# Scales from sums of squares by a product with ones, and half of w_in's sums split in place

## The chip, the cores and the metric

The kernel runs on one core of a Trainium2 chip. The metric is the device time of one execution in microseconds. A core has five engines with a queue of instructions each, which run in order: PE (TensorE, matrix products, with PEld for its weight loads), DVE (VectorE), ACT (ScalarE), POOL (GpSimd) and SP (SyncE, which here only issues DMAs). They wait for one another through semaphores. PSUM holds the results of products, SBUF the operands.

## The reference, cut to what matters

```python
scores = scale * (q @ k.T)                       # 4 batches, 8 heads, 576 rows, 64 wide
scores = where(scores >= max(scores) - tau, scores, -1e9)
x = softmax(scores) @ v                          # 2304 tokens, 512 wide
x = ((x @ w1) * (x @ w2)) @ w3 @ w_out           # moe, 1024 wide inside
h = x @ w_in                                     # moe2, 2048 wide inside
out = where(h > 0, h, exp(min(h, 0)) - 1) @ w_out2
```

## The kernel before

The kernel has five stages, one after the other, with overlap at their ends: attention, with the two products a and b of the first MoE and g = a·b (to 468 us); M = w3·w_out of the first MoE as one matrix (to 513); **the x2 stage**, x2 = g·M (to 630); and **MoE2** (to 1022).

The weights come in as 64-bit numbers. A chunk of 128 x 1024 is converted in four operations, which `conv_ops` gives: `top` on ACT, `rest` and `sign` (bit operations) and `join` on DVE. A product in full precision is three products of halves: a tile is split into a high half, a rounded copy, and a low half, the difference. For 16-bit halves the tile is first scaled by a power of two, which depends on its largest element. The scales are numbers that all 128 partitions need, while a maximum over a row gives one number for each partition.

Before the change a maximum over partitions is made by `everywhere` (L984): SP stores the column to DRAM (`mx_dr`, L988), loads it back as a row into every partition (`mxb`, L991), and DVE reduces it (L994). `power` (L978) makes a power of two of it.

The x2 stage runs over NB = 6 blocks of 384 tokens (the order is `JS`) and NK = 4 parts of 128 columns: 24 units with 24 products each (L1321), with x2 in PSUM (`x2`, four buffers). After the fourth unit of a block the g of the next block is split, in eight parts on ACT (`sl`, L325) and eight on DVE (L326), and the g of the block after that is loaded by SP (`th` from `g_dr`, L1128). ACT copies each x2 unit, the first eight into `bq` (L1361), the others into one of two buffers `x2s` (L1364), which SP stores (L1365). `x_size` (L1200) takes the maximum of a unit on DVE. `sums`, `high_b` and `low_b` make the sums of x2 quarters that MoE2's scheme needs and split them (`tq`, `so`).

Beside this, `win_jobs` converts w_in in eight chunks, in four pairs q. Each pair gives seven matrices (four of them sums, `s1` to `s4`, made on GpSimd in `both`), and SP stores all seven to DRAM (`wi_dr`, L1241). `size` takes the chunk's maximum on DVE (L1265). A list of jobs is worked off, one or two after each unit. At the stage's end the scale of all of w_in is made, again by `everywhere`.

MoE2 multiplies 2 x 2 blocks by seven products where eight would be needed. It runs in 24 steps s = (p, f): p is one of three thirds of the tokens, f one of eight parts of w_in. A step has seven products h (L1482), each of six matmuls; ACT takes the first from PSUM (`m1`, L1523), DVE adds up the others (`sum_of`, L1508), elu is made from the sums on ACT and DVE (L1409 to L1420), and the results are kept for the output products o (L1433), which fill in five at a time behind each product of the next step. In the first eight steps the parts of w_in come from DRAM: SP loads `wr`, GpSimd scales it (L1304), ACT makes the high half (L1307), GpSimd the low one (L1310), two at a time from `after`. In steps 0 to 3 four chunks of the last w_out are converted as well (`wo_steps`, with the maximum at L1021, the scaled copy at L1031 and its halves at L1032 and L1033). At step 4 their largest maximum is read (`seen`), and `h_scale` sets the scales of all three thirds.

The order on each engine is that of the program; nothing reorders it behind.

## Time and profile before

| | |
|---|---|
| median of three runs | 1027.48 us (1025.41 to 1027.63) |
| profiled execution | 1027.93 us, span 1026.1 us |
| PE busy | 948.0 us, 92% |
| PEld busy | 693.3 us, 68% |
| DVE busy | 778.3 us, 76% |
| ACT busy | 549.3 us, 54% |
| POOL busy | 444.2 us, 43% |
| mean granted clock of TensorE | 0.982 |

The span runs from the first instruction to the last; the execution's own time is 1.8 us more. A share of busy time is a mean over stages which have different limits. So the rows below are read by stage: how long a stage took, how long each engine was busy in it, and, on the engine that was idle, what ended its wait. In the chain that ended last each step is followed back to what released it. [...]

### The profile page before, as it was taken

Reading aid. Unit: us, or ns where it says so; the run is one execution under the profiler, and the core shown is the slowest. Engines: PE = TensorE matmul, PEld = TensorE weight load, DVE = VectorE, ACT = ScalarE, POOL = GpSimd, SP = SyncE. Lnnn points to the kernel's source line nnn. Section 1 sums busy time; section 2 is a strip of 40 time slices with the busy share of each in tenths; the row PEclk is TensorE's granted clock in tenths of the full one; section 3 lists DMA queues with packets and bytes.
Section 4 is the critical chain, followed back from the end, with each engine's and each line's share of the span. In section 5 each row is a group of like instructions: output and inputs, shape, how many; then the busy total and the mean of one; then the engine's idle time right before and its main releaser. Section 6 shows DMA issues by size and latency. Waiting matters only on the chain. (4 is left out here: it accounts for less than half of the span.)

```text
span 1026.1 us, 17137 instructions
## 1 busy us (share of the span) xinstructions
PE 948.0 (92%) x6074; PEld 693.3 (68%) x6074; DVE 778.3 (76%) x1448; ACT 549.3 (54%) x945; POOL 444.2 (43%) x608
## 2 busy tenths in 40 slices
PE   7889999989899999999999687687799999999998
PEld 4456788868799998997799686343355555555554
DVE  6889876888678785788968574888788677776664
ACT  5877776877666674454544233455455333443333
...
GB/s 261 148 129 168 153 156 141 169 169 176 179 203 185 202 135 160 280 214 263 206 180 268 158 198 226 154 124 36 60 31 1 124 2 1 1 63 1 1 1 62
DMA packets 167282, 138.18 MB, mean 135 GB/s; under 512 B 118332, under 2 KB 153884, under 8 KB 162588
## 3 DMA queue, kind: packets, MB, share of 16 engines
...
## 5 line engine op out<-in xcount | busy, mean ns | idle before, releaser
L681 PE MATMUL ab<-x,W 128*128 128x256 f32 (+1 forms) x1536 | 223.8, 298 | 6.3 <-DVE g L696 5.2
L1482 PE MATMUL h<-so,WI 128*128 128x384 f16 x1008 | 196.6, 333 | 32.1 <-DVE th L1508 18.6
L681 PEld LDWEIGHTS ab<-x,W 128*128 128x128 f32 x1536 | 207.6, 188 | 15.5 <-DVE g L696 6.2
L1433 PE MATMUL o<-WO,gg 128*128 128x512 f16 x864 | 214.3, 381 | 0.0
L1482 PEld LDWEIGHTS <-WI 128*128 128x128 f16 x1008 | 100.0, 99 | 121.3 <-issue 39.6
L1508 DVE SCALAR_TENSOR_TENSOR th<-h,back,th 128x384 f32<-128x384 f32 x168 | 100.8, 613 | 72.6 <-PE h L1482 72.0
L1433 PEld LDWEIGHTS <-gg 128*128 128x128 f16 x864 | 84.9, 98 | 86.0 <-issue 2.1
L526 DVE SCALAR_TENSOR_TENSOR e<-s,st,e 128x576 f32<-128x576 f32 x144 | 115.2, 808 | 24.1 <-ACT e L520 22.4
L537 POOL TENSOR_TENSOR hl<-e,hl 128x512 f16<-128x512 f32 x94 | 110.8, 1179 | 24.9 <-ACT hl L533 18.4
L502 DVE TENSOR_REDUCE st<-s 128x1 f32<-128x576 f32 x144 | 106.0, 750 | 17.5 <-PE s L492 10.1
L1321 PE MATMUL x<-sl,M 128*128 128x384 f32 x576 | 105.7, 346 | 11.1 <-ACT sl L325 4.4
L1410 ACT ACTIVATE et<-et 128x384 f32<-128x384 f32 x96 | 49.1, 511 | 120.7 <-DVE et L1409 120.7
L1321 PEld LDWEIGHTS x<-sl,M 128*128 128x128 f32 x576 | 103.7, 195 | 13.0 <-ACT sl L325 4.7
L1415 ACT ACTIVATE gg<-th,c_by 128x384 f16<-128x384 f32 x96 | 58.9, 613 | 74.0 <-DVE th L1413 73.8
L520 ACT ACTIVATE e<-s,st 128x576 f32<-128x576 f32 x108 | 78.4, 737 | 25.5 <-POOL st L510 16.6
L492 PE MATMUL s<-qk 128*128 128x288 f32 x480 | 83.1, 306 | 5.3 <-DVE e L526 4.4
L492 PEld LDWEIGHTS s<-qk 128*128 128x128 f32 x480 | 67.9, 189 | 14.0 <-issue 7.7
L533 ACT ACTIVATE hl<-e 128x576 f16<-128x576 f32 x94 | 63.1, 681 | 23.6 <-DMA pt<-hl 10.9
L1413 DVE SCALAR_TENSOR_TENSOR th<-et,th 128x384 f32<-128x384 f32 x96 | 59.4, 618 | 14.8 <-ACT et L1410 14.2
L1420 DVE SCALAR_TENSOR_TENSOR gg<-th,c_by,gg 128x384 f16<-128x384 f32 x96 | 62.9, 655 | 0.2 <-ACT gg L1415 0.2
L1310 POOL TENSOR_TENSOR WI<-wr,WI 128x256 f16<-128x256 f32 x56 | 41.9, 748 | 22.7 <-ACT WI L1307 22.7
L480 PE MATMUL s<-qkp 128*64 128x288 f32 x288 | 42.2, 427 | 7.1 <-ACT pt L578 3.7
...
## 6 DMA issues: line engine op xcount, KB each, us to landing
...
```

What stands on the lines that cost most here:

```text
L492: T.matmul(s[:, n, :HS], q, k[:, c:c + HS], start=(x == 0), stop=(x == len(ops) - 1))
L502: V.tensor_reduce(st[i][:, 0:1], sc[i][:, :, :HS], axis=AX.XY, op=ALU.max if plain else ALU.min, negate=plain)
L520: A.activation(et[i], sc[i][:, :, :HS], AF.Exp, bias=st[i][:, k:k + 1], scale=esc if plain else -1.0)
L526: V.scalar_tensor_tensor(et[i], sc[i][:, :, :HS], st[i][:, 1:2], et[i], op0=ALU.is_ge if p < NPL else ALU.is_le, op1=ALU.mult, accum_out=s ...
L533: A.activation(hl[i][:, :S], et[i].rearrange("p a b -> p (a b)"), AF.Copy)
L537: G.tensor_tensor(t[:, S + 64:], e[:, :512], t[:, :512], op=ALU.subtract)
L681: T.matmul(o[:, :w], wf[:, m, wx, kt, :], x[:, xx, :], start=(kt == 0 and k == 0), stop=(kt == NK - 1 and k == 2),)
L1321: T.matmul(o[:, :TB], M[:, f, mx, e * P:(e + 1) * P], gh[j, f][:, gx, :], start=(k == 0), stop=(k == 23),)
L1420: V.scalar_tensor_tensor(h[:, 1, :], x, c["by"], h[:, 0, :], op0=ALU.mult, op1=ALU.subtract)
L1433: T.matmul(po[j, t], dst["h"][:, gx, t * P:(t + 1) * P], WO[f // 2 % 4][:, f // 8, f % 2, wx, :], start=(first and k == 0), stop=(stop and ...
L1482: T.matmul(o[:, :TB], w[:, wx, kt, :], bs[k][:, kt, xx, :], start=(i == 0), stop=(i == 5),)
L1508: V.scalar_tensor_tensor(x, a, back[:, p:p + 1], b, op0=ALU.mult, op1=ALU.add)
```

## The change

- A scale is no longer made of a maximum, but of the root of a sum of squares: `root` halves the exponent of the sum. `square` makes a chunk's sum, on ACT for the first chunk of a pair of w_in and for w_out, on DVE for the second of a pair. `x_size` is a square on ACT, in place in PSUM, with a sum.
- The sum over partitions is a product with a matrix of ones (`total`), which lands in unused columns of a PSUM tile that is in use; DVE reads it after the next unit or product. `everywhere` stays for the maximum of w_out's scales, twice, with its load apart from its store.
- Each pair q of w_in has a scale of its own. For q = 0 and 1 (f = 0 to 3) `direct` splits the seven matrices where they stand, in the x2 stage: ACT copies with scale into the high half, DVE makes the low half one unit behind. They are no longer stored to and loaded from DRAM, nor scaled on GpSimd. For q = 2 and 3 the way is the old one, with five splits a step.
- The jobs of the x2 stage have fixed units (`slot`). One more chunk of w_out is converted there; three are left for steps 0 to 3. GpSimd's low half of a w_out chunk comes later (`behind`).
- The last maximum of w_out is read after the second product of step 4 and not ahead of its first sum; the scales of the second and third third of the tokens are made in step 5.

The diff, cut to its core:

```diff
+        def square(o, eng):
+            x, u = c["w"].bitcast(F32), c["u"]
+            if eng is A:
+                A.activation(u, x, AF.Square, accum_out=o)
+            else:
+                V.scalar_tensor_tensor(u, x, 1.0, x, op0=ALU.mult, op1=ALU.mult, accum_out=o)
+
+        return [top, rest, sign, join, high, low, lambda: c["w"].bitcast(F32), square]
...
-    def power(o, x, floor, by):
-
-        V.tensor_scalar(o.bitcast(I32), x.bitcast(I32), 0x7F800000, None, op0=ALU.bitwise_and)
-        V.tensor_scalar(o, o, floor, by, op0=ALU.max, op1=ALU.mult)
+    def root(o, x, floor, by):
+
+        V.tensor_scalar(
+            o.bitcast(I32), x.bitcast(I32), 1, 0x7F800000, op0=ALU.logical_shift_right, op1=ALU.bitwise_and
+        )
+        V.tensor_scalar(o, o, by * 2.0 ** 64, by * floor, op0=ALU.mult, op1=ALU.max)
 
     def everywhere(x):
 
@@ -986,14 +1004,15 @@
         nr[0] += 1
         d = drp.tile([P, k], F32, name=f"mx_dr{n}")
         SP.dma_start(d, x)
-        t = rawp[0].tile([P, 2 * P], F32, tag="mxb", name=f"mxb{n}", bufs=1)
-        flat = d.rearrange("(o p) k -> o (p k)", o=1)
-        SP.dma_start(t[:, :P * k], flat.to_broadcast([P, P * k]))
+        t = rawp[0].tile([P, P], F32, tag="mxb", name=f"mxb{n}", bufs=1)
+
+        def load():
+            SP.dma_start(t[:, :P * k], d.rearrange("(o p) k -> o (p k)", o=1).to_broadcast([P, P * k]))
 
         def read(o):
             V.tensor_reduce(o, t[:, :P * k].rearrange("p (a k) -> p k a", k=k), axis=AX.X, op=ALU.max)
 
-        return read
+        return load, read
...
-            V.tensor_reduce(raw_[:, c], ops[6](), axis=AX.X, op=ALU.max, apply_absolute_value=True)
-            power(two[:, c], raw_[:, c], LEAST, 2.0 ** -13)
+            root(two[:, c], raw_[:, c], LEAST, 2.0 ** -13)
             V.reciprocal(to[:, c], two[:, c])
...
-            G.tensor_tensor(t[:, :, 1, :], x2, t[:, :, 0, :], op=ALU.subtract)
-
-        return [[ops[0], ops[1]], [ops[2]], [ops[3], size], [halves]]
+            behind.append(lambda: G.tensor_tensor(t[:, :, 1, :], x2, t[:, :, 0, :], op=ALU.subtract))
+            if q % 4 < 2:
+                lows()
+
+        def lows():
+            while behind:
+                behind.pop(0)()
+
+        return [
+            [ops[0], ops[1], lows], [ops[2]], [ops[3], lambda: ops[7](raw_[:, c], A)], [size, halves]
+        ]
...
     def x_size(x, e, o):
-        V.tensor_reduce(xm[:, 4 * x + e:4 * x + e + 1], o, axis=AX.X, op=ALU.max, apply_absolute_value=True)
-
-    def x_sizes(p, o):
-        V.tensor_reduce(o, xm[:, 8 * p:8 * p + 8], axis=AX.X, op=ALU.max)
+        A.activation(o, o, AF.Square, scale=ROOM, accum_out=xm[:, 4 * x + e:4 * x + e + 1])
+
+    def total(o, x):
+
+        T.matmul(o[:, TB:TB + x.shape[1]], ones, x, start=True, stop=True)
+
+        def read(t, n):
+            V.tensor_reduce(
+                t, o[:, TB:TB + x.shape[1]].rearrange("p (n k) -> p n k", n=n), axis=AX.X, op=ALU.add
+            )
+
+        return read
...
+    def w_scale(q):
+        t = slice(q, q + 1)
+        root(w_two[:, t], wg[:, t], LEAST, 1.0)
+        V.tensor_scalar(w_to[:, t], w_two[:, t], 2.0 ** -11, None, op0=ALU.mult)
+        V.reciprocal(w_to[:, t], w_to[:, t])
...
+        def direct(k):
+            if q not in WIP:
+                WIP[q] = wp.tile([P, 2, NC, 2, 256], F16, tag=f"W{4 + 2 * q}", name=f"WI{q}")
+                for s_ in range(2):
+                    WI[2 * q + s_] = WIP[q][:, s_].rearrange("p k x (t c) -> p k x t c", t=2)
+            t, x, by = WIP[q][:, :, k], c[names[k]], w_to[:, q:q + 1]
+            A.activation(t[:, :, 0, :], x, AF.Copy, scale=by)
+            while behind:
+                behind.pop(0)()
+            behind.append(lambda: V.scalar_tensor_tensor(
+                t[:, :, 1, :], x, by, t[:, :, 0, :], op0=ALU.mult, op1=ALU.subtract
+            ))
+
+        def conv(key, ops, i):
+            col = wm[:, 2 * q + i:2 * q + i + 1]
+            return [ops[0], ops[1]], [ops[2], lambda: next_load(key), ops[3], lambda: ops[7](col, (A, V)[i])]
+
+        at = 5 * q
+        for i, ops in enumerate((ca, cb)):
+            for n, fns in enumerate(conv(keys[i], ops, i)):
+                slot[at + 2 * i + n] += fns
+        slot[at + 4].append(both)
+        if q > 1:
+            slot[at + 5].append(all_out)
+        else:
+            order = (1, 4, 6, 3, 0, 2, 5)
+            for n, k in enumerate(order):
+                slot[at + 6 + n // 2].append(call(direct, k))
+            slot[at + 10].append(lambda: behind.pop(0)())
+
+    slot = [[] for _ in range(NB * NK + 1)]
...
     for q in (2, 6, 3, 7):
         cs = wo_steps(q)
-        cs[2].append(lambda key=("wo2", q): next_load(key))
+        cs[1].append(lambda key=("wo2", q): next_load(key))
         jobs += cs
-    LATE = 16
-
-
+    for n in (19, 20, 22, 23):
+        slot[n].append(lambda: run_jobs(1))
+
+    USEQ = [(f, k) for f in range(4, NH) for k in range(NC)]
...
+            if n == 9:
+                seen = total(o, xm[:, 0:8])
+                reads.append(lambda seen=seen: (seen(xg[:, 0:1], 1), x_scale((0,))))
+            for q in range(4):
+                if n == 5 * q + 5:
+                    seen = total(o, wm[:, 2 * q:2 * q + 2])
+                    reads.append(lambda q=q, seen=seen: (seen(wg[:, q:q + 1], 1), w_scale(q)))
...
+            if n == 2:
+                seen[0]()
+            if n == 4:
+                seen[1](o_two[:, 0:1])
+            if n == 22:
+                V.tensor_reduce(w_two[:, 4:5], w_two[:, :4], axis=AX.X, op=ALU.max)
+                back_scale((0,))
                 h_scale((0,), o_two[:, 0:1])
...
+            if unsized:
+                x_size(*unsized.pop())
+            unsized.append((x, e, o[:, :TB]))
             if x == 2:
                 sums(e)
+            if x == 3 and e:
+                low_b(e - 1, 0)
             if x == 3 and e < 3:
                 high_b(e, 0)
-                low_b(e, 0)
-            if x == NB - 1 and e == 0:
-                for _ in range(NUR[0]):
-                    load_u()
-            if x == NB - 1 and e in (2, 3):
-                for _ in range(NUS[0] // 2):
-                    split_u()
-            for _ in range(1 + (x * NK + e in (0, 2))):
-                if len(jobs) > LATE:
-                    run_jobs(1)
-    run_jobs(len(jobs) - LATE)
-    while unsized:
-        x_size(*unsized.pop(0))
+            if x == NB - 1 and e == NK - 1:
+                for k in (3, 4):
+                    low_b(k, 0)
+            for fn in slot[n]:
+                fn()
+    x_size(*unsized.pop())
...
-            for _ in range(2):
-                if ns[0] < s * NC + k + sum(NUS):
-                    split_u()
-            while nu[0] < min(ns[0] + sum(NUR) - 2, len(USEQ)):
+            while ns[0] < min(max(5 * s + k + 1 - (k > 2) - (k > 5), (s - 4) * NC + k + 6), len(USEQ) + 2):
+                split_u()
...
+            seen(xg[:, 1:3], 2)
             x_scale((1, 2))
-        if s == NH // 2:
-            seen(o_two[:, 1:2])
-            V.reciprocal(shift, o_two[:, 1:2])
-            V.tensor_scalar(shift, shift, o_two[:, 0:1], None, op0=ALU.mult)
-            h_scale((0, 1, 2), o_two[:, 1:2])
-        run_jobs(2 * (s < NH // 2))
+            back_scale((1, 2))
+        run_jobs(int(s < NH // 2))
         after(0)
...
+        if s == NH // 2:
+            seen[1](o_two[:, 1:2])
+            V.reciprocal(shift, o_two[:, 1:2])
+            V.tensor_scalar(shift, shift, o_two[:, 0:1], None, op0=ALU.mult)
+            h_scale((0,), o_two[:, 1:2])
+        if s == NH // 2 + 1:
+            h_scale((1, 2), o_two[:, 1:2])
         after(1)
...
-            for h in (1, 2):
-                x_sizes(h, xg[:, h:h + 1])
-            seen = everywhere(xg[:, 1:3])
+            seen = total(ph[0], xm[:, 8:24])
         if s == NH // 2 - 1:
             V.tensor_reduce(o_two[:, 1:2], cols("wo_two", 8), axis=AX.X, op=ALU.max)
             seen = everywhere(o_two[:, 1:2])
+        if s == NH // 2 - 1 and behind:
+            behind.pop(0)()
         after(4)
...
         lows["22"][2]()
+        if s == NH // 2 - 1:
+            seen[0]()```

On DVE in the x2 stage, the rows ahead of the splits of g after the fourth block (units 11 to 15; `tq` and `so` are sums of x2 and their halves, `w_win` a chunk, `WI` the split sums of w_in). Before:

```order
L1208 TENSOR_SCALAR x_to_6750<-x_two_6749 128x1
L1209 RECIPROCAL x_to_6750<-x_to_6750 128x1
L1189 SCALAR_TENSOR_TENSOR so0_6726<-bq_6729,x_to_6750,so0_6726 128x2x384
L343 TENSOR_SCALAR w_win6_7285<-raw_win6_7070 128x1024
L1200 TENSOR_REDUCE xm_6747<-x2_1_3_7188 128x1
L1189 SCALAR_TENSOR_TENSOR so1_6727<-tq1_6731,x_to_6750,so1_6727 128x2x384
L347 TENSOR_SCALAR w_win6_7285<-raw_win6_7070 128x1024
L350 SCALAR_TENSOR_TENSOR w_win6_7285<-u_win6_7283,w_win6_7285 128x1024
L1265 TENSOR_REDUCE wm_6751<-w_win6_7285 128x1
L1200 TENSOR_REDUCE xm_6747<-x2_4_0_7247 128x1
L1189 SCALAR_TENSOR_TENSOR so2_6728<-bq_6729,x_to_6750,so2_6728 128x2x384
L326 TENSOR_TENSOR sl0_6387<-th0_6391,sl0_6387 128x384
```

And now:

```order
L1318 SCALAR_TENSOR_TENSOR WI1_7255<-s1_1_7147,w_to_6744,WI1_7255 128x2x256
L1318 SCALAR_TENSOR_TENSOR WI1_7255<-s4_1_7153,w_to_6744,WI1_7255 128x2x256
L347 TENSOR_SCALAR w_win6_7300<-raw_win6_7110 128x1024
L1214 SCALAR_TENSOR_TENSOR so0_6724<-bq_6727,x_to_6740,so0_6724 128x2x384
L1318 SCALAR_TENSOR_TENSOR WI1_7255<-s3_1_7151,w_to_6744,WI1_7255 128x2x256
L1318 SCALAR_TENSOR_TENSOR WI1_7255<-w_win1_6973,w_to_6744,WI1_7255 128x2x256
L351 TENSOR_SCALAR w_win6_7300<-raw_win6_7110 128x1024
L354 SCALAR_TENSOR_TENSOR w_win6_7300<-u_win6_7298,w_win6_7300 128x1024
L372 SCALAR_TENSOR_TENSOR u_win6_7298,wm_6741<-w_win6_7300 128x1024
L1214 SCALAR_TENSOR_TENSOR so1_6725<-tq1_6729,x_to_6740,so1_6725 128x2x384
L1318 SCALAR_TENSOR_TENSOR WI1_7255<-w_win1_6973,w_to_6744,WI1_7255 128x2x256
L327 TENSOR_TENSOR sl0_6382<-th0_6386,sl0_6382 128x384
```

Subtractions of `direct` stand between the operations on the chunk and on x2, and the sizes of x2 are gone from DVE.

On ACT in the x2 stage, the rows ahead of the splits of g after the second block (unit 7; `bq` is a copy of x2, `xm` the sums of squares). Before:

```order
L336 ACTIVATE u_win1_6951<-raw_win1_6792 128x1024
L1361 ACTIVATE bq_6729<-x2_3_1_6955 128x384
L321 DMA raw_win2_6983<-in_win 128x2048
L1361 ACTIVATE bq_6729<-x2_3_2_6987 128x384
L336 ACTIVATE u_win5_7014<-raw_win5_6854 128x1024
L325 ACTIVATE sl0_6387<-th0_6391 128x384
```

And now:

```order
L337 ACTIVATE u_win1_6971<-raw_win1_6815 128x1024
L1425 ACTIVATE bq_6727<-x2_3_2_6975 128x384
L1225 ACTIVATE x2_3_1_6943,xm_6737<-x2_3_1_6943 128x384
L1315 ACTIVATE WI0_7007<-s2_0_6937,w_to_6744 128x2x256
L1315 ACTIVATE WI0_7007<-s1_0_6935,w_to_6744 128x2x256
L322 DMA raw_win2_7012<-in_win 128x2048
L370 ACTIVATE u_win1_6971,wm_6741<-w_win1_6973 128x1024
L326 ACTIVATE sl0_6382<-th0_6386 128x384
```

The size of the unit before, two direct copies and the square of a chunk now stand ahead of the splits.

On DVE at the start of step 4 (`o_two` is w_out's largest scale, `h0_4_1` the second product of the step). Before:

```order
L994 TENSOR_REDUCE o_two_6755<-mxb3_8364 128x1
L1531 RECIPROCAL shift_6760<-o_two_6755 128x1
L1532 TENSOR_SCALAR shift_6760<-shift_6760,o_two_6755 128x1
...
L1219 TENSOR_SCALAR c_by_6759<-wo_two_5778,up_6757 128x8
L1508 SCALAR_TENSOR_TENSOR th1_6392<-h0_4_1_8465,back_6756,th0_6391 128x384
L1420 SCALAR_TENSOR_TENSOR gg12_0_3_8434<-th5_6396,c_by_6759,gg12_0_3_8434 128x384
```

And now:

```order
L1571 SCALAR_TENSOR_TENSOR th1_6387<-h0_4_1_8409,back_6746,th0_6386 128x384
L1482 SCALAR_TENSOR_TENSOR gg12_0_3_8397<-th5_6391,c_by_6749,gg12_0_3_8397 128x384
L1013 TENSOR_REDUCE o_two_6745<-mxb1_8330 128x1
L1601 RECIPROCAL shift_6750<-o_two_6745 128x1
L1602 TENSOR_SCALAR shift_6750<-shift_6750,o_two_6745 128x1
L1260 TENSOR_SCALAR out_by_6748<-x_two_6739,w_two_6743 128x1
...
L1264 TENSOR_SCALAR c_by_6749<-wo_two_5776,up_6747 128x8
```

The reduction of what the load brought now stands behind the sum of the second product, and one group of scales follows it in place of three.

## Rows read from the trace of the kernel before

**Rows 1.** Engine busy time by stage: from:to, length, engines (instructions), clock, DMA share, GB/s.

```profile
440.00:468.30 28.30, 24.18 (x197) 23.39 (x196) 22.99 (x31) 15.07 (x20) 11.28 (x5) 1.00 0.59 204
513.00:629.80 116.80, 105.75 (x577) 103.56 (x575) 76.61 (x117) 41.53 (x77) 25.82 (x18) 0.94 0.59 194
629.80:663.50 33.70, 18.22 (x76) 8.39 (x76) 24.70 (x46) 18.43 (x35) 24.00 (x34) 0.80 0.67 206
663.50:719.20 55.70, 45.55 (x229) 22.74 (x229) 47.69 (x80) 29.07 (x55) 36.46 (x41) 0.97 0.27 88
719.20:728.00 8.80, 2.66 (x12) 1.15 (x11) 5.38 (x22) 1.01 (x3) 5.32 (x10) 0.88 0.36 114
```

**Rows 2.** Timeline of TensorE, x2 stage: start, length, work, idle before and its releaser.

```profile
513.01 62.84 PE L1321 MATMUL x<-sl,M 128*128 128x384 f32 x360
579.69 5.76 PE L1321 MATMUL x<-sl,M 128*128 128x384 f32 x24 [3.83 <-DVE xm L1200]
589.87 0.66 PE L1321 MATMUL x<-sl,M 128*128 128x384 f32 x1 [4.42 <-ACT sl L325]
```

**Rows 3.** Timeline of SP's DMA queue, x2 stage.

```profile
560.98 0.68 SPq L988 DMA_DIRECT2D mx_dr<-xg  x1
571.11 0.33 SPq L991 DMA_DIRECT2D mxb<-mx_dr  x1
571.53 0.38 SPq L1365 DMA_DIRECT2D x_dr<-x2s  x1
```

**Rows 4.** Timeline of ACT, x2 stage.

```profile
576.18 0.49 ACT L1364 ACTIVATE x2s<-x 128x384 f32<-128x384 f32 x1 [11.69 <-PE x L1321]
```

**Rows 5.** The chain that ended last, in order of time, around step 4 and behind.

```profile
709.89 7.02 DMA mx_dr<-o_two
716.93 5.03 DMA mxb<-mx_dr
...
750.36 1.29 PE o L1433 x6
...
764.96 1.29 PE o L1433 x6
```

**Rows 6.** Groups by line: count, busy us, mean ns, idle before and its releaser.

```profile
L1307 ACT ACTIVATE WI<-wr 128x256 f16<-128x256 f32 x56 | 22.1, 408 | 25.2 <-POOL wr L1304 24.2 <-DVE wo_two L980 0.7
L1200 DVE TENSOR_REDUCE xm<-x 128x1 f32<-128x384 f32 x24 | 12.7, 545 | 0.0
L433 ACT ACTIVATE v<-vr 128x640 f16<-128x640 f32 x14 | 10.2, 730 | 1.5 <-PE pv L639 1.4
L1031 ACT ACTIVATE w_wo<-w_wo,wo_to 128x1024 f32<-128x1024 f32 x8 | 9.1, 1143 | 11.0 <-DVE wo_to L1023 11.0
L436 PE MATMUL s<-am,spread 128*128 128x1 f32 x28 | 4.0, 212 | 0.0
```

**Rows 7.** Timeline of DVE, x2 stage.

```profile
526.77 6.56 DVE L326 TENSOR_TENSOR sl<-th,sl 128x384 fp32r<-128x384 f32 x8 [0.94 <-ACT sl L325]
540.37 0.77 DVE L343 TENSOR_SCALAR w_win<-raw_win 128x1024 uint16<-128x1024 uint16 x1 [6.10 <-DMA wi_dr<-w_win]
542.34 1.23 DVE L350 SCALAR_TENSOR_TENSOR w_win<-u_win,w_win 128x1024 int32<-128x1024 int32 x1
545.85 3.83 DVE L326 TENSOR_TENSOR sl<-th,sl 128x384 fp32r<-128x384 f32 x8
577.53 1.02 DVE L1189 SCALAR_TENSOR_TENSOR so<-bq,x_to,so 128x768 f16<-128x768 f32 x1 [2.26 <-ACT so L1185]
```

**Rows 8.** Timeline of DVE, steps 1 to 4 of MoE2.

```profile
663.50 0.60 DVE L1508 SCALAR_TENSOR_TENSOR th<-h,back,th 128x384 f32<-128x384 f32 x1
667.06 1.22 DVE L1021 TENSOR_REDUCE wo_raw<-w_wo 128x1 f32<-128x1024 f32 x1
722.06 0.28 DVE L994 TENSOR_REDUCE o_two<-mxb 128x1 f32<-128x128 f32 x1 [2.89 <-DMA mxb<-mx_dr]
727.96 0.61 DVE L1508 SCALAR_TENSOR_TENSOR th<-h,back,th 128x384 f32<-128x384 f32 x1
```

124 lines of the change are left out of this document (57 added, 67 removed).

## The prediction

> **What bounds the kernel now.** I read the table by stage first: it cuts the span at the ends of the stages. From 728 us on TensorE is busy 98% of the time and nothing in the change touches its work there; the chain that ended last runs through the output products alone, and two of its markers, 750.36 and 764.96, give the steady period of one step of MoE2, 14.60 us [rows 5]. So a gain or a loss can only come from the stretch before. There TensorE is idle in five places [rows 1]: 4.1 us at the tail of the first MoE (28.30 less 24.18), 11.05 us in the x2 stage (116.80 less 105.75), 15.5 us from the start of MoE2 to the second sum of step 1 (33.70 less 18.22), 10.2 us in what is left of steps 1 to 3 and 6.1 us at the start of step 4. It also runs slower there: the granted clock is 0.94 in the x2 stage and 0.80 in the first part of MoE2, against 1.00 in the stretch ahead.
>
> The x2 stage is 24 units of 24 products. The row of 360 products without a gap gives 62.84/360 x 24 = 4.19 us for a unit, 100.5 for the stage [rows 2]; it took 116.8, so 16.3 us are lost: 11.05 idle and about 5.2 in products that run slowly after the idle stretches. The two large gaps are 3.83 and 4.42 [rows 2]. Their cause stands on the DMA queue of SP: the store of the column of maxima was issued at 560.98, its read-back had to wait for it until 571.11, and the store of x2 and the loads of g stood behind it [rows 3]; ACT's copy of an x2 unit then waited 11.69 us [rows 4] (the row names TensorE, but its buffer was still held by the store on SP).
>
> In the first four steps of MoE2 the bound is DVE: in steps 1 to 3 it is busy 47.69 of 55.70 us, TensorE 45.55 [rows 1], where three steps at the steady period would be 43.8. At step 4 the chain holds a store and a load of one number per row, 7.02 and 5.03 us [rows 5].
>
> **The change: the x2 stage.** The round trip through DRAM for the scale of x goes. In its place stand products with ones: TensorE needs about 0.25 us for each of the five that fall here (one pass is 212 ns [rows 6], a product of f32 has two that overlap with their weight load), 1.25 us in all, on the path. That alone would give back nearly all of the 16.3. But the change puts work into two queues that run in order: fourteen copies with scale on ACT, fourteen subtractions on DVE, squares in place of maxima, and the size of each x2 unit goes from DVE (545 ns each [rows 6]) to ACT.
>
> Prices. A copy of 512 elements on ACT lies between the one of 256, 408 ns, and the one of 640, 730 ns: 0.62. A square of 1024 with a sum: 1143 ns as the scaled copy of that size [rows 6], with some 0.2 for the sum. On DVE a subtraction of 512 elements is two thirds of the one of 768 (1.02): 0.68; a bit operation on 1024 is 0.77, a join 1.23 [rows 7]. For a square with its sum there is no row; it lies between the join and a join slowed as the splits are beside GpSimd, by 6.56/3.83: 1.2 to 2.1. I take 1.3, as the join is nearest in form.
>
> [...]
>
> What matters is what stands ahead of the splits of g, eight subtractions on DVE after every fourth unit (units 7, 11, 15, 19): TensorE's next unit needs them. A group of eight is 3.83 us alone and 6.56 when GpSimd works beside it [rows 7]. Between two such groups lie 16.8 us, 12.95 without the group.
> 1. Unit 7 to 8: on ACT two direct copies and the square stand ahead of the splits, and the square waits for a join which on DVE stands behind a subtraction. 0.49 + 0.6 + 2 x 0.62 + 1.2 for copies and square and about 2.2 for DVE's part: the splits start 5.7 after the end of unit 6 and give their first result some 1 us on, where TensorE was done with unit 7 at 4.2: it waits 2.5.
> 2. Unit 11 to 12: DVE has 12.2 of work and 2.7 of slowing by GpSimd in 12.95: 2 late.
> 3. Unit 15 to 16: six subtractions 4.1, a sum and two low halves of x 3.0, three bit operations 2.3, two joins 2.5, a square 1.3 and five small ones 0.8: 14.0. With 2.7 of slowing and about 4 of waiting for ACT (a top half 1.1, a square 1.3, three copies of 0.6), as the scale needs the square, the square the join, and the join the top half: 20.7, so 7.5 late.
> 4. Unit 19 to 20: nothing to speak of.
>
> Idle 12, the ones 1.25 and about 3 for slow products after each gap: 16.3, no different from now. The bounds: each wait is hidden and 3.8 are lost (a gain of 12.5), or the splits are later by 8 in sum (a loss of 8).
>
> **The start of MoE2.** The DRAM round trip for w_in's scale and the first loads of w_in's sums are gone; half of w_in is already split when MoE2 begins. DVE was busy 24.70 us up to the second sum of step 1, which ended this stretch at 663.50 [rows 8], 33.7 after its start. Taken off are one reduction of 1.22 [rows 8] and three sizes of 545 ns [rows 6]: 21.8. The waits for ACT between the parts of elu, about 2.4, stay. So 24.2, and 9.5 us are gained. It can't be below the 18.2 that TensorE works there (gain 15.5), and if the first product's copy on ACT is as late as now, some 3 us come back (gain 6.5).
>
> **Steps 1 to 3.** One chunk of w_out fewer is left for steps 0 to 3, three and not four: a chunk costs DVE two bit operations, a join and a reduction, 0.77 x 2 + 1.23 + 1.22 = 4.0, of which the reduction goes to ACT. Three reductions less are 3.7, and a quarter of the rest, over three steps, 2.0: 47.69 becomes 42.0. Of the 8.0 us that DVE idles there I keep 4.9, since GpSimd has five splits in a step for seven or more and its subtraction for w_out is put off. 46.9 is 8.8 below 55.70. The floor is TensorE's 43.8 (gain 11.9); if all 8.0 stay it is 50 (gain 5.7).
>
> **Step 4.** The load of the last maximum is now read behind the second product's sum instead of ahead of it, and scales for one third of the tokens are made there, not for all three. Before, 8.80 us passed [rows 1]: the wait of 2.89 [rows 8], 22 instructions of DVE with 5.38 [rows 1], up to the sum at 727.96 [rows 8]. Now the store is issued at product 4 of step 3 and the load at product 6; 12.05 us of transfers [rows 5] meet 5 products of 2.1, so a wait of 1.5 is left (0 to 4), then 8 small operations, 1.7, and sums of 1.9: 5.1, a gain of 3.7 (1 to 5).
>
> **The tail of the first MoE** has 4.1 idle [rows 1], part of it behind DVE's reductions of w_out chunks, which become squares on ACT: I take 1 (0 to 2).
>
> **Sum.** 0 + 9.5 + 8.8 + 3.7 + 1 = 23. The profiled execution took 1027.93 us for a span of 1026.1, which is 0.45 above the median of 1027.48: 1027.93 - 23 = 1004.9, and against the median 1004.5.
>
> **Rivals.**
> - The x2 stage runs clean. DVE and ACT have idle time in it in total (76.61 and 41.53 busy of 116.80 [rows 1]; with the moved work about 73 and 68), and a wait of one of the splits may be hidden by the other engine's lead. Then 12.5 more come off: 992. Against it speaks the order: the work stands ahead of the splits, not behind them.
> - The x2 stage gets worse by about 20, as more of the fourteen pairs fall ahead of splits while GpSimd works: the gain is nearly eaten, 1024.
> - The slower side: splits come as late at all five boundaries as in the third case above, 7.5 each. 37.5 idle, 5 for slow products and 1.25: 43.8 lost in place of 16.3, 27.5 more, against 23 won: 1032. It decides from the point where the stage loses 39 in all. DVE's idle total speaks against it, as only two boundaries have many of the pairs ahead of them.
> - The change doesn't do what it says for MoE2: DVE is still late by GpSimd's work, steps 1 to 3 give nothing and the start 6.5: 1016. It lies in the forecast's range.
>
> **How the numbers follow.** Forecast 0.60 (with the last rival in it), clean stage 0.27, nearly eaten 0.06, slower 0.07. Adding the ends of the unknown costs: the forecast alone goes from 996 to 1016; the clean case reaches down to 988. 988 to 1017 leaves out some 0.2: below 988 0.06, above 1017 0.14. A measurement of this kernel tells 0.2%, 2 us, from no change: faster is the forecast, the clean case and half of the nearly eaten one, 0.90; same 0.03; slower 0.07.
>
> **What would show it.** The x2 stage's length (116.8 by the forecast, 104 if clean), with TensorE's gaps ahead of units 8, 12 and 16, waiting for splits on DVE or ACT; no store and load of one column on SP between units 10 and 12; the second sum of step 1 some 24 us after the stage's end; 47 from there to the end of step 3; and 5 at the start of step 4. It would be wrong if TensorE's gaps in x2 are gone, or if a join or a square holds the splits at each boundary, or if DVE in steps 1 to 3 is as late as before.

## The result

The changed kernel took 1010.14 us (median of four runs, 1007.98 to 1010.91), the kernel before 1026.45 in the runs beside them (1024.96 to 1027.63): a ratio of 0.9839, interval 0.9815 to 0.9862, or 16.5 us less. The forecast was 1004.5 and 23 less, with 988 to 1017 as range: the direction and the range held, the size was some 6 us too good.

The profiled execution took 1010.8 us for a span of 1009.0, clock 0.986. Busy time of the engines by stage (from:to, length, then PE, PEld, DVE, ACT, POOL, the granted clock, the DMA share and GB/s), with the stages cut as in [rows 1]; only the cut ahead of step 4's start is not quite the same event (719.2 before, where DVE begins to wait for the load, 705.0 now, at the second product's sum), so the two rows beside it are safest taken together. The row from 468.7 is M, which took 44.7 before (468.3 to 513.0):

```profile
440.00:468.70 28.70, 25.60 (x200) 25.12 (x198) 20.97 (x30) 17.45 (x24) 11.34 (x5) 0.94 0.62 207
468.70:514.90 46.20, 44.13 (x192) 35.93 (x193) 36.95 (x39) 23.28 (x33) 15.52 (x7) 1.00 0.66 233
514.90:637.50 122.60, 110.82 (x587) 107.51 (x585) 80.37 (x136) 68.51 (x148) 29.20 (x18) 0.93 0.57 184
637.50:658.90 21.40, 13.75 (x69) 6.99 (x68) 16.72 (x38) 14.02 (x26) 9.32 (x12) 0.92 0.41 133
658.90:705.00 46.10, 45.11 (x243) 23.55 (x242) 42.34 (x73) 29.27 (x55) 29.64 (x32) 1.00 0.23 71
705.00:711.00 6.00, 3.06 (x16) 1.45 (x15) 3.50 (x13) 1.02 (x3) 4.76 (x8) 1.00 0.27 84
711.00:1009.00 298.00, 293.30 (x1552) 152.21 (x1551) 211.46 (x417) 116.56 (x215) 6.12 (x9) 0.99 0.06 22
```

| stage | before | after | forecast of the difference | measured |
|---|---|---|---|---|
| tail of the first MoE, and M | 73.0 | 74.9 | -1 | +1.9 |
| x2 stage | 116.8 | 122.6 | 0 | +5.8 |
| start of MoE2 to the second sum of step 1 | 33.7 | 21.4 | -9.5 | -12.3 |
| from there to step 4 | 55.7 | 46.1 | -8.8 | -9.6 |
| start of step 4 | 8.8 | 6.0 | -3.7 | -2.8 |
| the rest | 298.1 | 298.0 | 0 | -0.1 |

So MoE2 gave 24.7 us, and two stages ahead of it took 7.7 back. In steps 1 to 3 TensorE is now busy 45.11 of 46.10 us: it has become the bound there. The x2 stage is longer than before although its large gaps are gone. The timeline of TensorE (start, length, work, idle before and what ended it) has the gaps in another place:

```profile
514.93 25.60 PE L1387 MATMUL x<-sl,M 128*128 128x384 f32 x144
...
550.90 0.44 PE L1387 MATMUL x<-sl,M 128*128 128x384 f32 x1 [1.82 <-ACT sl L326]
...
571.45 17.05 PE L1387 MATMUL x<-sl,M 128*128 128x384 f32 x95 [1.01 <-DVE sl L327]
590.59 0.38 PE L1229 MATMUL x<-wm,ones 128*128 128x2 f32 x2 [2.09 <-DVE u_win L372]
591.40 0.44 PE L1387 MATMUL x<-sl,M 128*128 128x384 f32 x1 [0.43 <-ACT sl L326]
595.74 1.33 PE L1387 MATMUL x<-sl,M 128*128 128x384 f32 x3 [3.90 <-DVE sl L327]
597.29 17.76 PE L1387 MATMUL x<-sl,M 128*128 128x384 f32 x92 [0.23 <-DVE sl L327]
616.31 0.44 PE L1387 MATMUL x<-sl,M 128*128 128x384 f32 x1 [1.26 <-ACT sl L326]
617.42 1.33 PE L1387 MATMUL x<-sl,M 128*128 128x384 f32 x3 [0.68 <-DVE sl L327]
```

With two pieces of 0.15 and 0.22 that are left out here they are 11.79 us, where the stage before had 11.05, all between 575.9 and 594.7: the 3.83 and 4.42 of [rows 2], 2.58 more for DVE's splits of g, and 0.22. Units 8, 12, 16 and 20 are late by 2.0, 1.0, 6.7 and 2.2 us. They wait for the splits of g, but the first 2.09 of the 6.7 fall on the product with ones, which waits for DVE's square of a chunk (`u_win`); unit 16's first product then waited for a split in any case, until 591.40. Behind the waits of units 8, 16 and 20 the granted clock falls (0.79 from 550 to 558, 0.62 from 594 to 602, 0.63 from 618 to 626); behind the 1.0 of unit 12 it does not (1.00 from 570 to 578). In windows of 4 us behind the gaps at 590 and 616 the granted clock is 0.50 in both:

```profile
594.00:598.00 4.00, 2.03 (x5) 1.53 (x6) 4.00 (x5) 2.12 (x5) 2.82 (x2) 0.50 0.18 51
618.00:622.00 4.00, 3.78 (x12) 3.27 (x11) 4.00 (x8) 3.08 (x7) 0.50 (x1) 0.50 0.67 262
```

24 units at 4.19 are 100.5 us; 122.6 less 100.5 and 11.8 of idle leaves 10.3: about 0.9 for the five products with ones (0.14 each where the next product follows at once, as from 540.37 to 540.51, and 0.38 for the one at 590.59) and 9.4 for slow products, where before it was 5.2.

### The profile page after: what moved, and what is told of

It is laid out like the page before. It is cut to its first block, busy times and chain, and to the rows that moved or that the text cites. A ratio compares the mean times of both kernels' runs of the same rounds, so it can differ in the third digit from the quotient of the medians.

```text
span 1009.0 us, 17082 instructions
## 1 busy us (share of the span) xinstructions
PE 948.3 (94%) x6086; PEld 697.7 (69%) x6086; DVE 760.4 (75%) x1445; ACT 572.1 (57%) x1003; POOL 408.7 (41%) x553
## 5 line engine op out<-in xcount | busy, mean ns | idle before, releaser
L1545 PE MATMUL h<-so,WI 128*128 128x384 f16 x1008 | 193.2, 329 | 11.0 <-ACT th L1586 5.7
L1545 PEld LDWEIGHTS <-WI 128*128 128x128 f16 x1008 | 99.4, 99 | 96.0 <-issue 15.6
L1571 DVE SCALAR_TENSOR_TENSOR th<-h,back,th 128x384 f32<-128x384 f32 x168 | 100.9, 614 | 79.8 <-PE h L1545 74.7
L1387 PE MATMUL x<-sl,M 128*128 128x384 f32 x576 | 110.6, 353 | 9.7 <-DVE sl L327 6.2
L1387 PEld LDWEIGHTS x<-sl,M 128*128 128x128 f32 x576 | 106.3, 198 | 12.6 <-DVE sl L327 8.3
L1475 DVE SCALAR_TENSOR_TENSOR th<-et,th 128x384 f32<-128x384 f32 x96 | 56.5, 589 | 6.9 <-ACT et L1472 6.2
L1482 DVE SCALAR_TENSOR_TENSOR gg<-th,c_by,gg 128x384 f16<-128x384 f32 x96 | 60.2, 627 | 0.2 <-ACT gg L1477 0.2
L1090 PE MATMUL m<-WO,w 128*128 128x512 f32 x192 | 44.4, 391 | 3.0 <-DVE M L1100 1.9
```

The source lines that it names most:

```text
L1387: T.matmul(o[:, :TB], M[:, f, mx, e * P:(e + 1) * P], gh[j, f][:, gx, :], start=(k == 0), stop=(k == 23),)
L1475: V.scalar_tensor_tensor(x, c["t"], -1.0, x, op0=ALU.add, op1=ALU.max)
L1545: T.matmul(o[:, :TB], w[:, wx, kt, :], bs[k][:, kt, xx, :], start=(i == 0), stop=(i == 5),)
L1571: V.scalar_tensor_tensor(x, a, bk, b, op0=ALU.mult, op1=ALU.add)
```

## The experiments

Each kernel is the changed one with the edit that is shown. Its time stands beside the runs of the kernel before on the same chip, and the ratio of those is what is compared, since the chips differ by some 3 us (before: 1029.12, 1028.57 and 1026.03). A thousandth is 1 us; the ratio of the changed kernel itself, 0.9839, has an interval of 2.4 to either side, and most of the others one of 2 to 3.5, so the difference of two kernels is known to some 4 us from the ratios. Under that, a reading rests on the stages in the traces. These scatter too, as there is one trace for each kernel: the x2 stage is the same program in the changed kernel and in two of the runs below, whose edits lie in the first MoE and in step 4, and it took 122.6, 122.9 and 118.6 us. The last of the three (from:to, length, PE, PEld, DVE, ACT, POOL, granted clock):

```profile
513.80:632.40 118.60, 107.97 (x587) 105.05 (x585) 79.13 (x136) 68.50 (x148) 29.95 (x18) 0.94 0.58 190
```

So a change of the x2 stage by less than some 4 us isn't shown by its length alone. The start of MoE2 scatters from 21.4 to 22.5 in the runs whose edits don't touch it, and the stretch from there to the third sum of step 4 from 52.0 to 53.3.

### What holds the x2 stage

**GpSimd held back.**

```diff
+        if q == 2:
+            hold = cols("hold")
+            slot[at + 7].append(lambda: G.tensor_copy(hold, xm[:, 16:17]))
-        slot[at + 4].append(both)
+        slot[at + (7 if q == 2 else 4)].append(both)
...
-            slot[at + 5].append(all_out)
+            slot[at + (7 if q == 2 else 5)].append(all_out)
```

> GpSimd's four sums for the third pair of w_in are held back until the size of unit 16 is there, and their stores with them. Theory: at 590 to 600 GpSimd slows what stands ahead of unit 16 on DVE: a low half takes 2.02 for 1.00, a subtraction 1.75 for 0.75, the eight splits 5.98 for 3.83, 4.2 us in all; without GpSimd beside it the gap of 3.90 us nearly goes, with a part of the slow clock behind it: 5 us less, 1005. Rival: DVE is late at that place by its order (the subtractions wait for ACT), the gap stays over 3 us and GpSimd's work falls beside the splits after unit 19: 1010 or a little more.

Measured: 0.9787 (0.9753 to 0.9821), 1007.28 us, 5 less than the changed kernel. The x2 stage fell to 113.1 us, by 9.5. The rows of DVE ahead of unit 16, in the changed kernel and then with GpSimd held back:

```profile
589.30 1.22 DVE L372 SCALAR_TENSOR_TENSOR u_win<-w_win 128x1024 f32<-128x1024 f32 x1
590.45 0.08 DVE L372 DVE_READ_ACCUMULATOR u_win<-w_win 128x1 f32 x1
590.45 2.02 DVE L1214 SCALAR_TENSOR_TENSOR so<-tq,x_to,so 128x768 f16<-128x768 f32 x1
592.39 1.75 DVE L1318 SCALAR_TENSOR_TENSOR WI<-w_win,w_to,WI 128x512 f16<-128x512 f32 x1
594.07 5.98 DVE L327 TENSOR_TENSOR sl<-th,sl 128x384 fp32r<-128x384 f32 x8
```

```profile
591.91 1.01 DVE L1214 SCALAR_TENSOR_TENSOR so<-tq,x_to,so 128x768 f16<-128x768 f32 x1
592.84 0.75 DVE L1318 SCALAR_TENSOR_TENSOR WI<-w_win,w_to,WI 128x512 f16<-128x512 f32 x1
593.50 3.83 DVE L327 TENSOR_TENSOR sl<-th,sl 128x384 fp32r<-128x384 f32 x8
```

The last three rows are together 9.75 and 5.59 us, and TensorE's gap of 3.90 became one of 0.56:

```profile
594.11 23.31 PE L1390 MATMUL x<-sl,M 128*128 128x384 f32 x119 [0.56 <-DVE sl L327]
```

The theory holds for the place. The product with ones still waits there, 2.35 us, and 0.23 more behind it, so unit 16 is late by 3.1 in place of 6.7. Two things came beside it: the gap ahead of unit 20 went too, and the start of MoE2 got 3.5 us longer (24.9). The second goes with the stores of the third pair, which now go out late: ACT's copies of x2 waited for their buffers, 4.46, 3.86 and 1.61 us from 615 to 632, and the first product's copy came at 637.14, 7.2 behind the end of the stage.

**Four buffers for the copies of x2.**

```diff
-                t = xwp.tile([P, TB], F32, tag="x2s", name=f"x2s{j}_{e}", bufs=2)
+                t = xwp.tile([P, TB], F32, tag="x2s", name=f"x2s{j}_{e}", bufs=4)
```

> Four buffers in place of two for the copies of x2 that are stored. Theory: ACT's copy of unit 18 waited 6.26 us for the store of unit 16, which sat behind w_in's stores, and held the splits after unit 19; with four buffers the gaps of 1.26, 0.68 and 0.22 us ahead of unit 20 go, and the slow clock behind them (0.50 from 618 to 622): the x2 stage is about 4 us shorter than 122.6, the time about 1006. Rival: the splits after unit 19 are late by DVE and GpSimd in any case, the stage stays at 122 and the time at 1010.

Measured: 0.9805 (0.9782 to 0.9828), 1009.78 us; the x2 stage 119.2, 3.4 less. In the changed kernel ACT's timeline has the wait of which the prediction knew nothing:

```profile
614.86 0.49 ACT L1428 ACTIVATE x2s<-x 128x384 f32<-128x384 f32 x1 [6.26 <-DMA x_dr<-x2s]
```

With four buffers ACT did not wait there, but 0.78 and 0.75 us of the 2.16 stayed, for DVE's splits. GpSimd's sums of the fourth pair ran beside these, from 613.69 to 619.91, and the eight took 8.22 us where they take 3.83 alone:

```profile
613.52 8.22 DVE L327 TENSOR_TENSOR sl<-th,sl 128x384 fp32r<-128x384 f32 x8 [1.15 <-ACT sl L326]
```

With GpSimd held back the splits at this place are slowed as well, but ACT did not wait for a buffer, they began 3 us ahead of the end of unit 19 and not 1.2 behind it, and there is no gap:

```profile
610.39 6.02 DVE L327 TENSOR_TENSOR sl<-th,sl 128x384 fp32r<-128x384 f32 x8
```

So the buffer and GpSimd both bear on unit 20, and neither run separates them. What the buffer alone costs isn't shown: 3.4 us lie within the scatter of the stage, and in the trace of 118.6 above the gap is 1.25 with two buffers.

**The second pair of w_in by DRAM.**

```diff
-        if q > 1:
+        if q > 0:
             slot[at + 5].append(all_out)
...
-    USEQ = [(f, k) for f in range(4, NH) for k in range(NC)]
+    USEQ = [(f, k) for f in range(2, NH) for k in range(NC)]
...
-(s - 4) * NC + k + 6), len(USEQ) + 2)
+(s - 2) * NC + k + 6), len(USEQ) + 2)
```

(`half_of` then puts f = 2 and 3 where `direct` had them.)

> The second pair of w_in goes the old way (stored to DRAM, loaded in MoE2, scaled and split there), the first stays split in place: seven copies on ACT and seven subtractions on DVE leave the x2 stage, fourteen splits come to steps 0 to 3. Theory: those subtractions are what makes units 12 and 16 late; the gaps of 1.01 and 6.65 us shrink to about 2 in all and the slow clock with them, 7 to 8 us off the stage; MoE2's steps 0 to 3 get about 4 back from GpSimd and ACT: about 1006. Rival: the splitting in place is where the gain of 24.7 us in MoE2 comes from, and half of it is lost, 12 us, against the 8: about 1014.

Measured: 0.9780 (0.9751 to 0.9808), 1006.54 us, 6 less. The x2 stage is 116.3, by 6.3 shorter. Ahead of unit 16 TensorE waits 2.04 us in place of 6.65, and the product with ones doesn't wait:

```profile
588.07 0.80 PE L1392 MATMUL x<-sl,M 128*128 128x384 f32 x3 [0.52 <-DVE sl L327]
589.63 0.79 PE L1392 MATMUL x<-sl,M 128*128 128x384 f32 x3 [0.76 <-DVE sl L327]
591.18 15.98 PE L1392 MATMUL x<-sl,M 128*128 128x384 f32 x89 [0.76 <-DVE sl L327]
```

Ahead of unit 12 the gap stayed (0.87 for 1.01), so for that unit the theory is wrong. MoE2 lost nothing: 21.4 us to the second sum of step 1 and 52.5 from there to the third sum of step 4, as in the changed kernel (21.4 and 52.0). The rival falls. Even the theory's own price of 4 us was too high.

**Both pairs by DRAM.** The same for q = 0, with eight buffers `wr` that are there in the x2 stage, loads after unit 20 and three splits in each of the last two units.

```diff
-        if q > 1:
+        if q >= 0:
             slot[at + 5].append(all_out)
...
-    USEQ = [(f, k) for f in range(4, NH) for k in range(NC)]
+    USEQ = [(f, k) for f in range(NH) for k in range(NC)]
...
-            while ns[0] < min(max(5 * s + k + 1 - (k > 2) - (k > 5), (s - 4) * NC + k + 6), len(USEQ) + 2):
+            while ns[0] < min(s * NC + k + 6, len(USEQ) + 2):
```

> Neither pair of w_in is split in place: all 56 matrices go by DRAM as before the change, eight buffers for the loads, the first six splits in the last two units of the x2 stage, seven in each step of MoE2; everything else as after the change. With the second pair alone undone, MoE2 lost nothing. Theory: the first pair is what the start of MoE2 needs, so the stretch from its start to the second sum of step 1 goes from 21.4 us back towards 33 (28 to 31), steps 1 to 3 get 3 to 5 longer by GpSimd, and the x2 stage gains 7: 1014 to 1018. Rival: the start was late by the scale of w_in alone, which had a round trip through DRAM at the stage's end; with a scale for each pair known early the old way costs MoE2 nothing, and the time is about 1003.

Measured: 0.9831 (0.9801 to 0.9862), 1010.37 us, no difference from the changed kernel that can be told. It is the sum of a gain and a loss: the x2 stage is 112.9 us, 9.7 less, with no gap ahead of units 8 and 12; the start of MoE2 28.6, 7.2 more, and the steps to the third sum of step 4 55.4, 3.4 more. TensorE's rows of MoE2's start show the theory's cause, waits for splits of w_in (0.50 on ACT, then 0.60 and 0.64 on GpSimd), and a later one, ACT's first copy (6.30, where the changed kernel has 4.26):

```profile
632.14 0.50 PE L1557 MATMUL h<-so,WI 128*128 128x384 f16 x2 [0.50 <-ACT WI L1380]
...
642.15 4.90 PE L1557 MATMUL h<-so,WI 128*128 128x384 f16 x18 [6.30 <-ACT th L1598]
```

The stages went as the theory said; its total didn't, as I had set the gain of the x2 stage at 7. Splitting half of w_in in place, the largest part of the change, is worth nothing in sum that these runs could tell (to some 4 us); by the ratios its first half is worth about 5, its second costs about 6.

**The size of x2 on DVE.**

```diff
-        A.activation(o, o, AF.Square, scale=ROOM, accum_out=xm[:, 4 * x + e:4 * x + e + 1])
+        V.scalar_tensor_tensor(
+            o, o, ROOM * ROOM, c, op0=ALU.mult, op1=ALU.mult, accum_out=xm[:, 4 * x + e:4 * x + e + 1]
+        )
```

(`c` is ACT's copy of the unit.)

> The size of each x2 unit, a square with a sum, is made on DVE (from PSUM and the copy in SBUF) and not on ACT; everything else as after. Theory: DVE is what stands ahead of the splits of units 12 and 16; with 0.55 us more in each unit both are 2 us later, and ACT's lead elsewhere doesn't count: 1013 to 1015. Rival: what DVE gets, ACT loses, and the splits wait for ACT first (units 8 and 20): 1009 to 1011.

Measured: 0.9808 (0.9776 to 0.9839), 1006.58 us: not slower; the x2 stage is 118.2. That it is faster isn't shown, as 118.6 came without this edit too. The theory falls, the time is below the rival's too. DVE is busy 90.44 us of the stage against 80.37, ACT 57.48 against 68.51:

```profile
517.30:635.50 118.20, 106.93 (x588) 104.19 (x587) 90.44 (x182) 57.48 (x104) 29.70 (x18) 0.96 0.59 190
```

Ten more us of DVE cost nothing. There is room for them in its waits for ACT: in the changed kernel DVE stands idle for 4.45 and 2.87 us ahead of subtractions of `direct`, which wait for ACT's copies. Unit 12 was later (2.69 for 1.01), unit 16 was not (6.17 for 6.65), ahead of unit 8 it was 1.34 for 1.97, and ahead of unit 20 the gap fell from 2.16 to 0.92: in all 11.12 of idle for 11.79, so what the stage lost is nearly all in slow products. ACT's row behind the second pair's scale shows a link that the order alone doesn't: ACT's square writes the PSUM tile in which the product with ones has landed, so it waits until DVE has read that (at 574.60), which stands behind the splits:

```profile
574.78 0.47 ACT L1225 ACTIVATE x<-x 128x384 f32<-128x384 f32 x1 [2.76 <-DVE wg L1232]
```

### Where the gain of MoE2 and of the scales comes from

**The first scale of x by DRAM.**

```diff
-                seen = total(o, xm[:, 0:8])
-                reads.append(lambda seen=seen: (seen(xg[:, 0:1], 1), x_scale((0,))))
+                pass
+            if n == 10:
+                V.tensor_reduce(xg[:, 0:1], xm[:, 0:8], axis=AX.X, op=ALU.add)
+                seen = everywhere(xg[:, 0:1])
+                seen[0]()
+                trip = seen
+            if n == 12:
+                trip[1](xg[:, 0:1], ALU.add)
+                x_scale((0,))
```

> The first scale of x is summed over partitions by the round trip through DRAM (a store, a load, a reduction on DVE) in place of the product with ones: issued at unit 10, read at unit 12, as before the change; everything else as after. Theory: it was the wait of SP's queue for that store that made the two large gaps before; put back it holds the stores of x2 and the loads of g again, and the x2 stage gets 4 to 8 longer: 1014 to 1018. Rival: the round trip was long (9.4 us for the store) only because w_in's stores were ahead of it, which are gone for the first two pairs; it is hidden now, and the time stays at 1010.

Measured: 0.9871 (0.9837 to 0.9905), 1014.62 us; the x2 stage 125.7, 3.1 more. SP's queue waited again, 8.7 us between the store's issue and the load's, though no store of w_in was ahead of it:

```profile
568.17 0.32 SPq L1006 DMA_DIRECT2D mx_dr<-xg  x1
576.85 0.32 SPq L1010 DMA_DIRECT2D mxb<-mx_dr  x1
```

In that wait the DMA engines moved next to nothing (a share of 0.03):

```profile
568.20:576.80 8.60, 7.45 (x43) 7.13 (x42) 8.47 (x15) 4.50 (x11) 3.01 (x2) 1.00 0.03 6
```

So the wait is nearly as long without w_in's stores, and that rival falls. The next store of x2 went out behind it, at 577.26; ACT waited 4.1 us for a buffer of x2 in that stretch, and the product with ones ahead of unit 16 waited 4.81 for 2.09. The mechanism is as the prediction read it in [rows 3, 4]. Its price in the changed kernel is some 3 us by the ratio and by the stage, both within what scatters here, and not the 11 of idle that it stood beside.

**Step 4 as before the change.** The reading of the largest scale, and all three groups of scales, stand ahead of the second product's sum again.

```diff
+        if s == NH // 2:
+            seen[1](o_two[:, 1:2])
+            ...
+            h_scale((0, 1, 2), o_two[:, 1:2])
         run_jobs(int(s < NH // 2))
         after(0)
```

> At step 4 the largest scale of w_out is read ahead of the second product's sum, and the scales of all three thirds of the tokens are made there, as before the change; everything else as after. Theory: the sum at 705.0 moves to 712, since it stands behind a wait of 2.3 and 4.0 of small operations; TensorE has only the output products of two products in hand, so 3 to 4 us are lost: 1013 to 1014. Rival: only the wait for the load counts, which is the same in both orders: 1010 to 1011.

Measured: 0.9890 (0.9849 to 0.9931), 1015.20 us, 5 more. From the second sum of step 1 to the third of step 4 it took 56.3 us for 52.0, and TensorE's gap is 7.98 where the changed kernel has 3.57:

```profile
705.20 0.29 DVE L1013 TENSOR_REDUCE o_two<-mxb 128x1 f32<-128x128 f32 x1 [4.45 <-DMA mxb<-mx_dr]
708.97 0.61 DVE L1571 SCALAR_TENSOR_TENSOR th<-h,back,th 128x384 f32<-128x384 f32 x1
```
```profile
709.64 2.08 PE L1545 MATMUL h<-so,WI 128*128 128x384 f16 x6 [7.98 <-DVE th L1571]
```

The theory holds: the stretch is longer by 4.3, clear of its scatter. The first products behind the gap take 2.08 in place of 1.14 us.

**All four late chunks of w_out in MoE2.**

```diff
-    for n in (19, 20, 22, 23):
-        slot[n].append(lambda: run_jobs(1))
...
-        run_jobs(int(s < NH // 2))
+        run_jobs(2 * (s < NH // 2))
         after(0)
```

> All four chunks of w_out that were left after the first MoE are converted in steps 0 to 3 of MoE2, as before the change, none in the x2 stage; everything else as after. Theory: the chunk in the x2 stage costs nothing there, and in steps 0 to 3 a fourth chunk is 2.8 us of DVE beside 40.7 busy of 43.9 in steps 1 to 3, and its waits: 3 to 5 us more, 1013 to 1015. Rival: TensorE's 14.6 a step hide it, 1010.

Measured: 0.9898 (0.9863 to 0.9933), 1016.56 us, 6 more by the ratio; in the trace the stretch to the third sum of step 4 is 3.3 longer (55.3), beyond its scatter, and the start of MoE2 1.0, within it. The theory holds for the steps. The profiled execution is one of the two longer of four (1018.72; the shorter ones are 1014.00 and 1014.39) and was late by 4.2 us when M began, ahead of anything that the edit changes, so the price is nearer to 3 than to the ratio's 6. Whether the chunk is free in the x2 stage isn't shown: 120.6 lies within the scatter.

**Squares of the early w_out chunks on DVE.**

```diff
-            [ops[0], ops[1], lows], [ops[2]], [ops[3], lambda: ops[7](raw_[:, c], A)], [size, halves]
+            [ops[0], ops[1], lows], [ops[2]], [ops[3], lambda: ops[7](raw_[:, c], A if q % 4 > 1 else V)], [size, halves]
```

> The squares of the four chunks of w_out that are converted ahead of the x2 stage are made on DVE and not on ACT. Theory: on ACT they stand ahead of the copies of a, which TensorE waits for at the tail of the first MoE (2.21 us at 460.18, then a clock of 0.76 to 0.81); with them on DVE the x2 stage starts 2 us earlier, at 513: about 1008. Rival: the wait there comes from the conversion as such, whichever engine makes the square, and the x2 stage starts at 515 as now: 1010.

Measured: 0.9823 (0.9786 to 0.9860), 1009.60 us, which tells nothing by itself. The profiled execution was a long one, late by 6 us when M began; in it M took 44.6 us to the start of the x2 stage, as before the change, where the changed kernel took 46.3. TensorE's last wait in M is 0.71 for 1.93, behind DVE's `M`.

### Together

**Second pair by DRAM, GpSimd held back, four buffers.** The three edits above in one kernel.

> Three of the edits together: the second pair of w_in by DRAM, GpSimd's sums of the third pair held until unit 16's size, four buffers for the stored copies of x2. Theory: the first takes the subtractions from ahead of unit 16, the second GpSimd's slowing, the third the copies' waits for stores, which took 3.5 us of the second's gain back at the start of MoE2 when it stood alone; the x2 stage is about 110 us, the rest as after: 12 less than after the change, 998 where that is 1010. Rival: the waits they take away are the same one, and the stores of three pairs crowd the queue: not better than the second pair by DRAM alone, 1004.

Measured: 0.9714 (0.9695 to 0.9734), 998.62 us, 12.8 less than the changed kernel, where the theory had 12. TensorE has two gaps in the x2 stage, 3.8 us, and its granted clock is 1.00 over the stage:

```profile
552.31 9.03 PE L1395 MATMUL x<-sl,M 128*128 128x384 f32 x48 [1.83 <-ACT sl L326]
...
572.27 16.77 PE L1395 MATMUL x<-sl,M 128*128 128x384 f32 x95 [1.99 <-DVE sl L327]
```
```profile
516.80:622.90 106.10, 102.13 (x587) 100.78 (x585) 73.69 (x129) 64.41 (x141) 30.02 (x19) 1.00 0.71 229
```

The stage lost 16.5 us against the changed kernel, 7.8 of idle and 8.7 of busy time: with the gaps most of the slow products went. That is 4 more than the theory had for it (110); M took 1.5 longer in this trace and the stretch to the third sum of step 4 1.3, so a part of the agreement is luck.

**ACT's first copy of MoE2 ahead.** To that kernel:

```diff
-    for k in (5, 6):
-        high_b(k, 0)
...
         A.activation(m1, o, AF.Copy, scale=bk)
+        if s == 0:
+            for k in (5, 6):
+                high_b(k, 0)
...
-    for n in (19, 20, 22, 23):
+    for n in (19, 20, 22):
...
-        run_jobs(int(s < NH // 2))
+        run_jobs(int(s < NH // 2) + (s == 0))
```

> The three edits that gave 998.6 together, and at the start of MoE2 ACT takes the first product from PSUM ahead of the scaled copies of a w_out chunk (2.2 us) and of two high halves of x2 (1.8 us). Theory: TensorE's gap of 4.26 us ahead of the third product falls to about 1, 3 us are gained: 995 to 996. Rival: the high halves and the chunk are late then, and the gap moves to the sixth product: 998 to 999.

Measured: 0.9692 (0.9670 to 0.9714), 994.70 us. The theory's gap went, and the rival's gap came: the wait of 4.26 is down to one of 0.29, and TensorE now waits 3.71 us a little later, behind DVE:

```profile
631.95 0.61 PE L1229 MATMUL h<-xm,ones 128*128 128x16 f32 x2 [3.71 <-DVE th L1577]
```

The start of MoE2 is 20.8 us for 21.7, so of the 2.2 in the ratio about 0.9 can be shown in the trace.

**With the early squares on DVE as well.**

> As the run with ACT's first copy ahead, and the squares of the four early chunks of w_out on DVE. Theory: in the trace with these squares on DVE the stretch from the start of M to the x2 stage was 44.6 us, against 45.8 to 47.8 in all the others with them on ACT; 2 us are gained: 993 to 994. Rival: that difference is scatter of the stage, the time is that of the run without it, 995 to 996.

Measured: 0.9670 (0.9639 to 0.9700), 992.26 us, the fastest kernel here, 34 us below the one before. From the start of M to the x2 stage it is 44.6 us again (46.2 in the run without the edit), so the early squares on ACT cost about 1.6 us there. The intervals of the two runs overlap; that part rests on the two traces with the edit, both 44.6, against 45.8 to 47.9 in the eleven without it.

## Why the prediction was right or wrong

**The waits of the x2 stage: right for three units, and by their mechanism; the fourth was missed.** Units 8, 12, 16 and 20 were to wait 2.5, 2, 7.5 and 0; they waited 2.0, 1.0, 6.7 and 2.2. That their sum of 12 came out at 11.8 is luck: 9.6 are the forecast's three, 2.2 were not foreseen. GpSimd's slowing makes 3.5 of the 6.7 ahead of unit 16, as without it 3.1 are left; the prediction had 2.7 for it. The subtractions ahead of the splits are shown as a cause for unit 16 by the run with the second pair by DRAM (2.0 left), and for units 8 and 12 by the one with both pairs by DRAM, where TensorE doesn't stop at all there. For unit 12 it is then the first pair's work, not the second's. That TensorE itself would stand at the product with ones, 2.09 us for a square, was not in the prediction, which had these products at 0.25 each; the splits came later anyhow. The wait ahead of unit 20 has two causes that the prediction lacks: ACT stood for 6.26 us behind a buffer of x2, and GpSimd worked beside the splits. This buffer had a row of its own in the trace before [rows 4], which I had read as the doing of the round trip alone.

**The slow products behind the gaps: the step that failed.** I put 3 us for them, without a working; they took 9.4. At the price of the trace before, 5.2 for 11.05 us of idle, the 12 would have had 5.6. There are three stretches now with a granted clock of 0.50 to 0.79 (550 to 558, 594 to 602, 618 to 626), and their 4.1 us more than before, with 0.7 more of idle and 0.9 for the products with ones, are the 5.8 that the stage is longer. A price for one gap the rows don't give: the 48 products behind the same wait of 1.83 us ahead of unit 8, which are 8.4 us at full pace, took 9.03 in the run with the three edits and 10.46 in the fastest kernel. And with step 4 as before, the x2 stage being the same program, the products behind a gap of 1.25 ahead of unit 20 ran nearly at full pace, 4.8 us for the unit's 24, which took 7.8 in the changed kernel. What decides between the two stays open.

```profile
547.99 10.46 PE L1395 MATMUL x<-sl,M 128*128 128x384 f32 x48 [1.83 <-ACT sl L326]
```
```profile
615.56 4.33 PE L1387 MATMUL x<-sl,M 128*128 128x384 f32 x23 [0.57 <-DVE sl L327]
```

**The tail of the first MoE, and M: wrong in sign.** I took a gain of 1 for DVE's reductions that leave. TensorE's idle time in the tail did fall by 1.0 (28.70 less 25.60, for 4.12), but its products took 1.4 longer, at a granted clock of 0.94 for 1.00. In M, which the prediction left alone, the idle time rose from 0.8 to 2.1 us. M before:

```profile
468.30:513.00 44.70, 43.92 (x192) 36.05 (x193) 39.38 (x44) 21.27 (x29) 16.23 (x7) 1.00 0.68 241
```

The squares that take the reductions' place stand on ACT; back on DVE they give M its 44.6 us. What I had not priced is the engine that the work moves to.

**The start of MoE2: right, and undersized.** 12.3 for 9.5. I took 2.9 us off DVE's work and kept 2.4 of its idle time: 21.8 and 2.4. It was 16.7 busy and 4.7 idle, so two errors cancel in part. GpSimd is busy 9.32 us there where it was 24.00, so less slowing by it is a likely reason for the first; no run shows it singly. By the run with both pairs by DRAM 7.2 of the 12.3 are the splits in place, of the first pair by the run that undoes the second alone; the rest came with that kernel too.

**Steps 1 to 4: right.** 12.4 measured for 12.5, 9.6 and 2.8 for 8.8 and 3.7; DVE's busy time in steps 1 to 3 was to be 42.0 and is 42.34. Undone one at a time, the reading at step 4 costs 4.3 us in the trace and the chunk of w_out 3.3.

**The rivals.** The clean stage (104 us) did not come, but can be had: 106.1 with three edits. The one in which the gain of x2 is eaten came in part. That the change does not do what it says for MoE2 is refuted. Half of w_in split in place is a part of what it does there: without it MoE2 gets 10.6 of the 24.7 us longer, but the x2 stage 9.7 shorter, so the time is the same.

**What the change is worth part by part**, from the runs that undo one thing, each to some 4 us: reading late in step 4, 5 us (4.3 in the trace); the chunk of w_out moved, 6 (3.3 in the steps); the product with ones for x, 3, not clear of the scatter; splitting in place, nothing in sum (first pair a gain, second a loss of 6); the size of x2 on ACT, no gain, perhaps a loss of 3. They add up to some 11 of the 16.5, which their intervals allow. What the scale for each pair of w_in gave was not measured by itself.

**The price of a square on DVE: right.** I took 1.3. The row at 589.30 above has 1.22 us and 0.08 for reading the sum, no more than the 1.23 of the join of the same size [rows 7], and the other three of its kind in the trace have the same. Both its sources are one tile, so the row prices that form alone.
